# Second passes of the last product: who makes the low parts of the weight sums of steps 1 and 2

## The chip, the cores and the metric

The kernel runs on one core of a Trainium2 chip. The metric is the device time of one launch in microseconds (us). Three timed runs of the kernel before the change took 1035.53, 1036.79 and 1036.57 us, so the median is 1036.57 us. One further execution was profiled; it took 1036.03 us, and its span from first to last instruction is 1034.2 us. All times below that stand in rows of the profile are microseconds from the start of that span.

## The reference

One input `x` (2048 rows of 640) goes through two branches, which are mixed row by row with a gate. Branch A is a Fourier mixing by matrix products, branch B a gated feed-forward layer.

```python
def reference(A_x, A_dft_seq_re, A_dft_seq_im, A_dft_hid_re, A_dft_hid_im, B_x, B_w_gate, B_w_up, B_w_down, gate_w):
    ...
        a = jnp.einsum("bsd,ed->bse", x, dft_hid_re)
        b = jnp.einsum("bsd,ed->bse", x, dft_hid_im)
        y = jnp.einsum("ts,bse->bte", dft_seq_re, a) - jnp.einsum("ts,bse->bte", dft_seq_im, b)
    ...
        return (_gelu(x @ w_gate) * (x @ w_up)) @ w_down
    x = A_x
    g = _sigmoid((x * gate_w).sum(-1, keepdims=True))
    a = _A_ref(x, A_dft_seq_re, A_dft_seq_im, A_dft_hid_re, A_dft_hid_im)
    b = _B_ref(x, B_w_gate, B_w_up, B_w_down)
    return g * a + (1 - g) * b
```

The change touches the last product of branch B, the product of the hidden activations with `w_down` (1728 by 640).

## The kernel before

Nearly every float32 matrix product is made of three matmuls on TensorE. Each operand is split into a high part in the format `fp32r` and a low part, which is what the high part leaves over; `mm3` multiplies high by high (line 99), high weight by low data (line 100) and low weight by high data (line 101). A matmul takes 128 by 128 weights and 128 by 512 data. The products are further arranged in the manner of Strassen: blocks of weights and of data are added and subtracted first, so that fewer products are needed.

The work follows in stages: the gate and up products with the gelu (to about 326 us), the sequence product of branch A (to about 724 us), then the product with `w_down` (724 to 908 us), and last the hidden product of branch A and the mixing. This text is about the third of these.

The product with `w_down` goes over two halves of the output (`tp` 0 and 1), in each over two passes (`b` 0 and 1), and in each pass over steps `k`: six of them (0 to 5) over pairs of blocks of the hidden dimension, and one, `NK` (6), for what is left over. The order in `kseq` is: in pass 0 the steps 0 to 6, in pass 1 the steps 0, 6, 1, 2, 3, 4, 5. Tiles are named by it: `kb0121l` is the low part of the data of half 0, pass 1, step 2, second pair of blocks; `kh` and `kl` are the high and low part of a step's weights, `kw` the weights as loaded, `kr` the data as loaded. Data of step 0 in pass 1 is called `kb0100` and `kb0101`. In the views of the profile numbers at the ends of names are left out.

One iteration of the loop over `kseq` does this: `load_k` of the step three ahead starts the loads (from SyncE's queue: weights `kw` of 128 and 384 KB, then two data tiles `kr` of 512 KB each); `split_k` of the step two ahead makes its high and low parts; `late` carries out what an earlier step left to be gated and stored (line 919 on VectorE, line 920 by a DMA that GpSimd issues); and `step_k` issues the products. In pass 1 the data is not used as loaded: VectorE makes four differences first (lines 826 to 829), 128 by 512 each. Then the high parts of the data are made by ScalarE (line 80) and the low parts by VectorE (line 83).

The weights of pass 1 are loaded as sums made earlier (`wsd`). For these, ScalarE writes the high part (`high`, line 80), then minus the weights into the tile for the low part (`negative`, line 91, which rounds to the same format), and then GpSimd issues a DMA that adds the loaded weights onto it (`left_of`, line 95). In pass 0, `split` does the same with ScalarE for the high part and VectorE for the low one (line 83).

ScalarE and VectorE carry out their work in the order of the program (`in_order`). TensorE, SyncE and GpSimd are set in order by the scheduler of the framework, by its own estimate of when things are ready.

The gate of each half passes through DRAM: sums over rows of `x` on VectorE (line 711), a sigmoid on ScalarE (line 687), a store issued by GpSimd (line 690), and a load of one broadcast row by SyncE (line 695). Loads that stand behind line 695 in SyncE's queue wait with it; those are the loads of steps 1, 2, 3 and on of pass 1.

Of the kernel before, what the change touches and what calls it, by code (L numbers as in the profile page):

```python
# [35 lines left out]
def kernel(  # L36
# [33 lines left out]
    def slot(dt, shape, name):  # L70
        return pool.tile(shape, dt, tag="s4", name=name, bufs=46)
# [7 lines left out]
    def high(hi, raw):  # L79
        nc.scalar.activation(hi, raw, AF.Copy)  # L80

    def low(hi, lo, raw):
        nc.vector.tensor_tensor(lo, raw, hi.bitcast(F32), op=ALU.subtract)  # L83

    def split(hi, lo, raw):
        high(hi, raw)
        low(hi, lo, raw)

    def negative(lo, raw):

        nc.scalar.activation(lo, raw, AF.Copy, scale=-1.0)

    def left_of(lo, raw):

        nc.gpsimd.dma_start(lo, raw, accum_op=ALU.add)
# [41 lines left out]
    def hl(name):  # L137
        return pair(F32R, f"{name}h"), pair(F32R, f"{name}l")

    def at(hilo, i):  # L140
        h, l = hilo
        return h[:, i], l[:, i]
# [676 lines left out]
    def split_k(i):  # L819
        tp, b, k = kseq[i]  # L820
        n = f"{tp}{b}{k}"
        r, raw = kraw.pop(i)
        sums = b and k < NK
        if sums:
            (b11, b12), (b21, b22) = ([v[:, q] for q in range(2)] for v in raw)
            tt(b11, b12, b11, op=ALU.subtract)
            tt(b12, b22, b12, op=ALU.subtract)
            tt(b22, b22, b11, op=ALU.subtract)
            tt(b21, b21, b22, op=ALU.subtract)
        B = []  # L830

        def right():
            B = []
            for q in range(2):
                v = hl(f"kb{n}{q}")
                split(*v, raw[q])
                B += [at(v, 0), at(v, 1)]
            return [B[q] for q in (0, 3, 1, 2)] if sums else B

        if k == NK and b:  # L840
            W = ktile.pop(("left", tp))
        elif k == NK:
            r, m, d = r
            tt(m[:, 5:7], m[:, 0:2], m[:, 2:4], op=ALU.subtract)
            tt(d[:, 0:2], d[:, 0:2], d[:, 2:4], op=ALU.subtract)
            tt(m[:, 5:7], m[:, 5:7], d[:, 0:2], op=ALU.add)
            B = right()
            c, l, a = (slot(F32R, [P, 8, P], f"k{v}{n}") for v in "cla")
            high(c[:, :7], m[:, :7])
            low(c[:, :7], l[:, :7], m[:, :7])  # L850
            high(a[:FR, 2:4], m[:FR, 2:4])
            low(c[FR:, 2:4], a[FR:, 2:4], m[FR:, 2:4])
            x = slot(F32R, [P, 8, P], f"kx{n}")
            split(x[:, 0:2], x[:, 2:4], r[:, 0:2])
            split(x[:, 4], x[:, 5], r[:, 4])
            mx = {"A22": (a[:, 2], a[:, 3])}
            for name, (u, v) in {"A12": (0, 1), "e5": (4, 4), "S4": (5, 6)}.items():
                mx[name] = [[w[q * FR : (q + 1) * FR, k] for w in (c, l)] for q, k in enumerate((u, v))]
            W = {"A11": [(x[:, q], x[:, 2 + q]) for q in range(2)]}, (x[:, 4], x[:, 5]), mx
            kraw["left", tp] = r, m  # L860
            ktile["left", tp] = W
        else:
            h, l = slot(F32R, [P, 8, P], f"kh{n}"), slot(F32R, [P, 8, P], f"kl{n}")
            if b:
                high(h, r)
                negative(l, r)
                left_of(l, r)
            else:
                split(h, l, r)
            names = ("A22", "S1", "S2", "S3") if b else ("A11", "A12", "e5", "S4")  # L870
            W = {name: (at((h, l), 2 * q), at((h, l), 2 * q + 1)) for q, name in enumerate(names)}
        ktile[i] = W, B or right()
# [143 lines left out]
    with in_order(ACT, DVE, PE):  # L1016
# [5 lines left out]
        for d in range(ND):  # L1022
# [3 lines left out]
            if d == 0:  # L1026
                a, b = halves
# [202 lines left out]
    with in_order(PE, ACT, DVE, POOL):  # L1230
        for f in range(1, NF):
# [36 lines left out]
            if f == 2:  # L1268
                k = len(fills) // 2
# [91 lines left out]
    for i, (j, ri, b, sp) in enumerate(cseq):  # L1361
# [70 lines left out]
        else:  # L1432
            if j == 1 and ri == 1 and sp >= 4:
                if sp < 7:
                    load_k(sp - 4)
                if 4 < sp < 7:
                    split_k(sp - 5)
# [55 lines left out]
    for i in range(len(kseq)):  # L1493
# [13 lines left out]
        if i + 2 < len(kseq):  # L1507
            split_k(i + 2)
# [243 lines left out]
```

## Time and profile before

| | |
|---|---|
| median of three timed runs | 1036.57 us |
| profiled execution, time | 1036.03 us |
| profiled execution, span | 1034.2 us |
| mean granted clock of TensorE | 0.993 |
| chain that ended last: TensorE | 90% |
| chain that ended last: DMA `kl<-kw` | 2% |
| HBM read, written | 191.69 MB, 57.69 MB |

The chain that ended last is followed back from the last instruction: at each step to what released it. Its 90% on TensorE says that the time is mostly the sum of the matmuls; its 2% on one DMA, named by output and input, says that somewhere TensorE stood for that transfer. A row of the view by time gives start, duration, engine, line, operation, output and inputs, and in brackets the idle time ahead of it and what ended it. A row of the view by windows gives the stretch, then busy time and number of instructions of PE (TensorE), PEld (its weight loads), DVE (VectorE), ACT (ScalarE) and POOL (GpSimd), then the granted clock, the share in which the DMA engines were busy, and what they moved in GB/s.

### The profile page before, as it was taken

What the parts mean: (1) busy time and instruction counts of PE and PEld (TensorE: products, weight loads), DVE (VectorE), ACT (ScalarE), POOL (GpSimd) and SP (SyncE); (2) the same over time, 40 slices, a digit from 0 to 9 for tenths busy, and PEclk for the clock granted to TensorE, in tenths of its full rate; (3) what the DMA queues carried; (4) which work ended last, traced back from release to release, by engine and by line L of the source; (5) the groups of instructions that cost most, each with busy time, mean ns of one, the idle gap of its engine ahead of it and who ended that gap; (6) DMA issues with size and microseconds to landing.
All of it is one profiled execution on the core that took longest, in us unless ns stands there. A gap on an engine that the chain in (4) does not pass through costs nothing.

```text
span 1034.2 us, 13182 instructions
## 1 busy us (share of the span) xinstructions
PE 1019.9 (99%) x4489; PEld 840.5 (81%) x4489; DVE 813.0 (79%) x1147; ACT 501.6 (48%) x636; POOL 169.3 (16%) x290
## 2 busy tenths in 40 slices
PE   9999999999999999999999999999997999899998
PEld 7888888888888888888888888888886887788887
DVE  8877765564748969978975988777987998797796
ACT  6644535354444744524444444344565637555340
POOL 0221111111110200132023102200211011011112
PEclk9999999999999999999999999999998999899999
DMA  8556364554577976798679768979969999997856
GB/s 310 153 195 219 110 193 132 179 156 153 162 222 251 275 217 211 240 373 299 200 257 397 281 213 285 397 253 312 357 223 330 393 340 347 332 398 220 268 150 99
DMA packets 92164, 261.28 MB, mean 253 GB/s; under 512 B 12160, under 2 KB 22528, under 8 KB 92096
## 3 DMA queue, kind: packets, MB, share of 16 engines
q1 hardware_dynamic: 66624, 180.78, 50.4%
q0 software_dynamic: 25184, 79.46, 26.1%
q8 instruction: 35, 0.57, 0.2%
q14 instruction: 33, 0.27, 0.1%
q10 hardware_dynamic: 288, 0.20, 0.1%
HBM read 191.69 MB, written 57.69 MB: 241 GB/s over the span
## 4 chain that ended last, share of the span: by engine, by line
PE 90%; DMA 3%; issue 3%; DVE 2%; POOL 1%; ACT 0%; SPq 0%; POOLq 0%; DVEq 0%; ACTq 0%
PE pX L101 7%; PE pX L99 7%; PE pX L100 7%; PE pZ L101 5%; PE pZ L100 5%; PE pZ L99 4%; PE pL L99 3%; PE pL L101 3%; PE pL L100 3%; PE pV L99 2%; PE pV L101 2%; PE pV L100 2%; DMA kl<-kw 2%; PE pY L99 1%; PE pR L99 1%
## 5 line engine op out<-in xcount | busy, mean ns | idle before, releaser
L80 ACT ACTIVATE ch<-csa 128x1024 fp32r<-128x1024 f32 x32 | 34.0, 1062 | 79.0 <-DVE csa L767 74.4
L80 ACT ACTIVATE ch<-cra 128x1024 fp32r<-128x1024 f32 x32 | 33.9, 1059 | 46.9 <-DVE cl L83 14.2
L83 DVE TENSOR_TENSOR cl<-cra,ch 128x1024 fp32r<-128x1024 f32 x32 | 39.1, 1222 | 21.0 <-ACT ch L80 18.7
L415 POOL DMA_DIRECT2D hA<-s x48 | 26.2, 546 | 179.3 <-DVE s L582 160.2
L83 DVE TENSOR_TENSOR cl<-crb,ch 128x1024 fp32r<-128x1024 f32 x32 | 39.1, 1221 | 17.2 <-ACT ch L80 15.7
L100 PE MATMUL pL<-cl,xah 128*128 128x512 f32 x128 | 49.8, 389 | 0.0
L101 PE MATMUL pL<-ch,xal 128*128 128x512 f32 x128 | 49.8, 389 | 0.0
L99 PE MATMUL pL<-ch,xah 128*128 128x512 f32 x128 | 49.0, 389 | 0.0
L80 ACT ACTIVATE ch<-crb 128x1024 fp32r<-128x1024 f32 x32 | 33.8, 1057 | 30.6 <-DVE cl L83 8.5
L571 DVE TENSOR_TENSOR s<-s,pX 128x512 f32<-128x512 f32 x24 | 16.4, 684 | 38.5 <-PE pX L101 38.5
L83 DVE TENSOR_TENSOR cl<-csa,ch 128x1024 fp32r<-128x1024 f32 x32 | 39.0, 1220 | 7.2 <-ACT ch L80 5.2
L146 ACT ACTIVATE s<-pX 128x512 f32<-128x512 f32 x41 | 24.2, 596 | 38.2 <-PE pX L101 37.6
L83 DVE TENSOR_TENSOR cl<-csb,ch 128x1024 fp32r<-128x1024 f32 x32 | 39.2, 1224 | 4.2 <-ACT ch L80 3.2
L80 ACT ACTIVATE ch<-csb 128x1024 fp32r<-128x1024 f32 x32 | 34.0, 1063 | 13.5 <-DVE csb L770 5.1
L557 ACT ACTIVATE s<-pZ 128x512 f32<-128x512 f32 x24 | 14.2, 597 | 52.1 <-PE pZ L101 35.3
L576 ACT ACTIVATE s<-s 128x512 f32<-128x512 f32 x24 | 15.1, 634 | 46.6 <-DVE s L575 46.6
L1352 POOL DMA_DIRECT2D uA<-c x8 | 4.3, 540 | 167.1 <-DVE c L1464 166.9
L80 ACT ACTIVATE kh<-kw 128x1024 fp32r<-128x1024 f32 x24 | 25.4, 1058 | 7.6 <-DMA kw<-wsd 7.5
L101 PEld LDWEIGHTS pL<-ch,xal 128*128 128x128 f32 x128 | 24.0, 188 | 5.0
L100 PEld LDWEIGHTS pL<-cl,xah 128*128 128x128 f32 x128 | 24.0, 188 | 5.0
L99 PEld LDWEIGHTS pL<-ch,xah 128*128 128x128 f32 x128 | 24.0, 188 | 5.0
L101 PE MATMUL pX<-ch,xal 128*128 128x512 f32 x64 | 24.9, 389 | 0.0
(3658 smaller groups left out, 3482.3 us busy)
## 6 DMA issues: line engine op xcount, KB each, us to landing
cra<-in_ct SPq DMA_DIRECT2D x64, 512.0 KB, 5.1
crb<-in_ct SPq DMA_DIRECT2D x64, 512.0 KB, 6.0
kr<-hA SPq DMA_DIRECT2D x48, 512.0 KB, 9.2
hA<-s POOLq DMA_DIRECT2D x48, 256.0 KB, 2.9
ux<-uA SPq DMA_DIRECT2D x24, 512.0 KB, 7.3
ux<-uT SPq DMA_DIRECT2D x16, 512.0 KB, 7.0
xq<-xp POOLq DMA_DIRECT2D x12, 512.0 KB, 5.1
xu<-xv POOLq DMA_DIRECT2D x12, 512.0 KB, 4.0
```

The source lines that it names most:

```text
L80: nc.scalar.activation(hi, raw, AF.Copy)
L83: nc.vector.tensor_tensor(lo, raw, hi.bitcast(F32), op=ALU.subtract)
L99: nc.tensor.matmul(ps, lh, rh, start=first, stop=False, skip_group_check=True)
L100: nc.tensor.matmul(ps, lh, rl, start=False, stop=False, skip_group_check=True)
L101: nc.tensor.matmul(ps, ll, rh, start=False, stop=last, skip_group_check=True)
L146: nc.scalar.activation(m, src, AF.Copy)
L415: nc.gpsimd.dma_start(to[:, i], src)
L557: nc.scalar.activation(s5, Z, AF.Copy)
L571: tt(s5, s5, X, op=ALU.add)
L576: nc.scalar.activation(s2, s2, AF.Gelu_apprx_tanh)
L1352: nc.gpsimd.dma_start(to[:, i], src)
```

## The change

In pass 1, steps 1 and 2 of both halves now make the low part of their weights as pass 0 does, with VectorE (`split`). Step 0 and steps 3, 4 and 5 keep ScalarE's negative and the adding DMA.

```diff
@@ -861,7 +861,7 @@
             ktile["left", tp] = W
         else:
             h, l = slot(F32R, [P, 8, P], f"kh{n}"), slot(F32R, [P, 8, P], f"kl{n}")
-            if b:
+            if b and k not in (1, 2):
                 high(h, r)
                 negative(l, r)
                 left_of(l, r)
```

So in all four instructions of line 91 leave ScalarE, four adding DMAs leave GpSimd, and four instructions of line 83 join VectorE.

The order on VectorE, half 0, from the end of the differences of step 1 (`kr0110`, `kr0111`) on. Before:

```order
L829 TENSOR_TENSOR kr0111_6544<-kr0111_6544 128x512
L83 TENSOR_TENSOR kb0110l_6615<-kr0110_6542,kb0110h_6614 128x1024
L83 TENSOR_TENSOR kb0111l_6619<-kr0111_6544,kb0111h_6618 128x1024
L919 TENSOR_TENSOR ks1000_6584<-ks1000_6584,gm5_6507 128x512
L919 TENSOR_TENSOR ks1001_6586<-ks1001_6586,gm5_6507 128x512
L919 TENSOR_TENSOR ksl000_6594<-ksl000_6594,gm5_6507 128x512
L919 TENSOR_TENSOR ksl001_6596<-ksl001_6596,gm5_6507 128x512
L826 TENSOR_TENSOR kr0120_6601<-kr0120_6601 128x512
L827 TENSOR_TENSOR kr0120_6601<-kr0121_6603,kr0120_6601 128x512
L828 TENSOR_TENSOR kr0121_6603<-kr0121_6603,kr0120_6601 128x512
L829 TENSOR_TENSOR kr0121_6603<-kr0121_6603 128x512
L83 TENSOR_TENSOR kb0120l_6677<-kr0120_6601,kb0120h_6676 128x1024
```

And now, from the same place on:

```order
L83 TENSOR_TENSOR kl011_6610<-kw011_6539,kh011_6609 128x1024
L83 TENSOR_TENSOR kb0110l_6614<-kr0110_6542,kb0110h_6613 128x1024
L83 TENSOR_TENSOR kb0111l_6618<-kr0111_6544,kb0111h_6617 128x1024
L919 TENSOR_TENSOR ks1000_6584<-ks1000_6584,gm5_6507 128x512
L919 TENSOR_TENSOR ks1001_6586<-ks1001_6586,gm5_6507 128x512
L919 TENSOR_TENSOR ksl000_6594<-ksl000_6594,gm5_6507 128x512
L919 TENSOR_TENSOR ksl001_6596<-ksl001_6596,gm5_6507 128x512
L826 TENSOR_TENSOR kr0120_6601<-kr0120_6601 128x512
L827 TENSOR_TENSOR kr0120_6601<-kr0121_6603,kr0120_6601 128x512
L828 TENSOR_TENSOR kr0121_6603<-kr0121_6603,kr0120_6601 128x512
L829 TENSOR_TENSOR kr0121_6603<-kr0121_6603 128x512
L83 TENSOR_TENSOR kl012_6671<-kw012_6598,kh012_6670 128x1024
```

The low part of the weights stands ahead of the two low parts of the data, in step 1 (`kl011`) and in step 2 (`kl012`), so all that follows on VectorE stands one and then two instructions further back.

On ScalarE the two rows of line 91 leave, and the next high part moves up. Half 0, steps 1 to 3, before:

```order
L80 ACTIVATE kh011_6609<-kw011_6539 128x1024
L91 ACTIVATE kl011_6610<-kw011_6539 128x1024
L80 ACTIVATE kb0110h_6614<-kr0110_6542 128x1024
L80 ACTIVATE kb0111h_6618<-kr0111_6544 128x1024
L80 ACTIVATE kh012_6671<-kw012_6598 128x1024
L91 ACTIVATE kl012_6672<-kw012_6598 128x1024
L80 ACTIVATE kb0120h_6676<-kr0120_6601 128x1024
L80 ACTIVATE kb0121h_6680<-kr0121_6603 128x1024
L80 ACTIVATE kh013_6717<-kw013_6660 128x1024
L91 ACTIVATE kl013_6718<-kw013_6660 128x1024
```

And now:

```order
L80 ACTIVATE kh011_6609<-kw011_6539 128x1024
L80 ACTIVATE kb0110h_6613<-kr0110_6542 128x1024
L80 ACTIVATE kb0111h_6617<-kr0111_6544 128x1024
L80 ACTIVATE kh012_6670<-kw012_6598 128x1024
L80 ACTIVATE kb0120h_6674<-kr0120_6601 128x1024
L80 ACTIVATE kb0121h_6678<-kr0121_6603 128x1024
L80 ACTIVATE kh013_6715<-kw013_6659 128x1024
L91 ACTIVATE kl013_6716<-kw013_6659 128x1024
```

The negative of step 3 (`kl013`) still stands behind the high parts of step 2's data, which wait for VectorE's differences.

On TensorE the scheduler gives steps 1 and 2 the same order as before, but step 3 another one. The start of step 3, half 0, before:

```order
L99 MATMUL kX000_6201<-kb0131h_6726,kh013_6717 128x512
L100 MATMUL kX000_6201<-kb0131l_6727,kh013_6717 128x512
L101 MATMUL kX000_6201<-kb0131h_6726,kl013_6718 128x512
L99 MATMUL kX001_6202<-kb0131h_6726,kh013_6717 128x512
L100 MATMUL kX001_6202<-kb0131l_6727,kh013_6717 128x512
L101 MATMUL kX001_6202<-kb0131h_6726,kl013_6718 128x512
L99 MATMUL kQ010_6630<-kb0130h_6722,kh013_6717 128x512
```

And now:

```order
L99 MATMUL kX000_6201<-kb0131h_6724,kh013_6715 128x512
L99 MATMUL kX001_6202<-kb0131h_6724,kh013_6715 128x512
L99 MATMUL kQ010_6629<-kb0130h_6720,kh013_6715 128x512
L100 MATMUL kQ010_6629<-kb0130l_6721,kh013_6715 128x512
L99 MATMUL kQ011_6630<-kb0130h_6720,kh013_6715 128x512
L100 MATMUL kX000_6201<-kb0131l_6725,kh013_6715 128x512
L101 MATMUL kX000_6201<-kb0131h_6724,kl013_6716 128x512
```

The first matmul that reads the low part of the weights (`kl013`) stood third in the step and now stands seventh. In step 4 it stood tenth and now stands twelfth; step 5 is as it was, with the low part twelfth. SyncE's loads keep their order. In half 1 all of this is the same.

## The prediction

> **What bounds the kernel now.** First the page's busy times, then the list of TensorE's waits.
>
> ```profile
> PE 1019.9 (99%) x4489; PEld 840.5 (81%) x4489; DVE 813.0 (79%) x1147; ACT 501.6 (48%) x636; POOL 169.3 (16%) x290
> PE kX L101 <- DMA kl<-kw: 10.2, 4, 3.9
> PE idle L1020 <- PEq L1740: 0.8, 1, 0.8
> ```
>
> TensorE is the bound, and but for the start it waits in one place alone: four times, 10.2 us in all, for the adding DMA that makes `kl`. The change acts on that DMA. Its waits in order of time, half 0 and then half 1, each step's first row beside them:
>
> ```profile
> 780.85 0.39 PE L99 MATMUL kX<-kb0111h,kh 128*128 128x512 f32 x1
> 783.10 0.50 PE L101 MATMUL kX<-kb0111h,kl 128*128 128x512 f32 x1 [1.63 <-DMA kl<-kw]
> ...
> 788.23 0.39 PE L99 MATMUL kX<-kb0121h,kh 128*128 128x512 f32 x1
> 792.79 0.79 PE L101 MATMUL kX<-kb0121h,kl 128*128 128x512 f32 x1 [3.94 <-DMA kl<-kw]
> ...
> 800.29 0.39 PE L99 MATMUL kX<-kb0131h,kh 128*128 128x512 f32 x1
> 805.73 0.62 PE L99 MATMUL kQ<-kb0140h,kh 128*128 128x512 f32 x2
> ...
> 873.07 0.39 PE L99 MATMUL kX<-kb1111h,kh 128*128 128x512 f32 x1
> 880.35 0.39 PE L99 MATMUL kX<-kb1121h,kh 128*128 128x512 f32 x1
> 884.00 0.79 PE L101 MATMUL kX<-kb1121h,kl 128*128 128x512 f32 x1 [3.04 <-DMA kl<-kw]
> 891.94 0.39 PE L99 MATMUL kX<-kb1131h,kh 128*128 128x512 f32 x1
> ```
>
> The waits lie in steps 1 and 2, the two that are changed. A step of 24 matmuls without a wait takes 805.73 - 800.29 = 5.44 us, 0.227 a matmul. Step 1 of half 0 takes 788.23 - 780.85 = 7.38, so it loses 1.94; step 2 takes 12.06 and loses 6.62. In half 1 step 1 loses 7.28 - 5.44 = 1.84 and step 2 11.59 - 5.44 = 6.15. That is **16.55 us**, more than the 10.2 of idle time. The rest is in the clock:
>
> ```profile
> 780.78:784.19 3.41, 1.78 (x9) 1.14 (x8) 3.31 (x6) 1.47 (x2) 1.92 (x3) 1.00 1.02 355
> 787.61:791.02 3.41, 1.24 (x6) 0.70 (x4) 3.34 (x4) 2.92 (x3) 0.43 (x1) 1.00 1.06 302
> 791.02:797.85 6.83, 5.06 (x12) 3.99 (x13) 2.49 (x5) 2.00 (x3) 0.86 (x1) 0.50 1.06 289
> 872.94:876.35 3.41, 1.86 (x9) 1.22 (x8) 3.30 (x5) 2.88 (x3) 0.85 (x1) 1.00 1.02 357
> 879.77:883.18 3.41, 1.20 (x6) 0.66 (x4) 3.33 (x4) 2.90 (x3) 0.09 (x1) 1.00 1.03 261
> ```
>
> After each long wait the granted clock is 0.50 for 6.83 us. Of the 3.41 us ahead of that TensorE was busy 1.24 in half 0 and 1.20 in half 1. With 1.78 and 1.86 busy, after the short waits, the clock stayed at 1.00. So a wait of about 1.6 us costs itself alone, one of 3 us costs up to 3.4 us (half of 6.83) on top.
>
> [...]
>
> **The change, part by part.** What it takes from ScalarE and GpSimd is worth nothing by itself, since TensorE never waits for either's busy time. What counts is when VectorE now has `kl`, what it has later for that, and when the next adding DMA, step 3's, lands.
>
> ```profile
> 777.29 1.23 DVE L83 TENSOR_TENSOR kb0111l<-kr,kb0111h 128x1024 fp32r<-128x1024 f32 x1
> ...
> 783.01 0.69 DVE L829 TENSOR_TENSOR kr<-kr 128x512 f32<-128x512 f32 x1
> 784.87 1.22 DVE L83 TENSOR_TENSOR kb0121l<-kr,kb0121h 128x1024 fp32r<-128x1024 f32 x1
> ...
> 807.29 1.22 DVE L83 TENSOR_TENSOR kl<-kw,kh 128x1024 fp32r<-128x1024 f32 x1
> 808.43 1.22 DVE L83 TENSOR_TENSOR kb1000l<-kr,kb1000h 128x1024 fp32r<-128x1024 f32 x1
> 783.78 1.06 ACT L80 ACTIVATE kb0121h<-kr 128x1024 fp32r<-128x1024 f32 x1 [0.44 <-DVE kr L829]
> 785.70 1.04 ACT L91 ACTIVATE kl<-kw 128x1024 fp32r<-128x1024 f32 x1
> 783.36 0.90 POOL L95 DMA_DIRECT2D kl<-kw  x1 [1.41 <-ACT kb0120h L80]
> 787.15 0.89 POOL L95 DMA_DIRECT2D kl<-kw  x1 [2.88 <-PE kR L101]
> 792.54 0.86 POOL L95 DMA_DIRECT2D kl<-kw  x1 [4.50 <-ACT kl L91]
> DMA to landing us min/median/max: 7.7/8.7/9.9
> ```
>
> A low part of a weight tile holds VectorE 808.43 - 807.29 = 1.14 us. *Half 0, step 1:* with `kl` ahead of it, the last data part, begun at 777.29, ends at 777.29 + 1.14 + 1.23 = 779.7, before TensorE asks at 780.85: nothing lost. *Step 2:* its last data part, begun at 784.87 now, comes after two more instructions of 1.14, less the 0.1 it stood for ScalarE: 787.05 to 788.3. TensorE asks for it one matmul into step 2, at 780.85 + 5.44 + 0.23 = 786.5. It waits **1.8 us**, short of the clock's price by the rows above. What VectorE delays behind this (gating, differences) is waited for by step 3 alone.
>
> *Step 3* keeps the adding DMA, and TensorE now comes to it earlier. Its line 91 on ScalarE stands behind `kb0121h`, which waits for VectorE's line 829, now 1.14 later; so 785.70 becomes 786.85. The issue followed line 91's start by 787.15 - 785.70 = 1.45, so it goes out at 788.3. Landings took 7.7 to 9.9 us; I take the median, 8.7: landed at 797.0. TensorE ends step 2 at 788.3 + 23 x 0.227 = 793.5 and by the new order has six matmuls before it reads `kl`, so it asks at 794.9: a wait of **2.1 us** (1.1 to 3.3 over the landings). It leaves TensorE busy for at least 3.4 - 2.1 = 1.3 us of a stretch of 3.4, between the rows with and without the clock's price; I take it without, since a stretch need not begin with the wait. *Step 4:* its issue at 792.54 becomes about 794.5, as VectorE's differences of step 3 are some 2.2 later; landed 803.2, asked for at 797.0 + (18 + 11) x 0.227 = 803.6: hidden, by little. Half 0 gains 8.56 - 1.8 - 2.1 = 4.7.
>
> ```profile
> 866.90 1.23 DVE L83 TENSOR_TENSOR kb1110l<-kr,kb1110h 128x1024 fp32r<-128x1024 f32 x1 [1.32 <-ACT kb1110h L80]
> 875.63 1.23 DVE L83 TENSOR_TENSOR kb1121l<-kr,kb1121h 128x1024 fp32r<-128x1024 f32 x1
> 876.45 1.05 ACT L91 ACTIVATE kl<-kw 128x1024 fp32r<-128x1024 f32 x1
> 877.90 0.89 POOL L95 DMA_DIRECT2D kl<-kw  x1 [1.48 <-ACT kl L91]
> ```
>
> *Half 1* is milder. VectorE stood 1.32 us for `kb1110h`, which was behind line 91 on ScalarE. With that gone, step 1's `kl` fits in the hole and what follows comes 1.32 - 1.14 = 0.2 earlier than before. Step 2 adds 1.14: its last data part ends at 875.63 + 0.94 + 1.23 = 877.8, asked for at 873.07 + 5.44 + 0.23 = 878.7. No wait. Step 3: issue at 877.7, landed 886.4; asked for at 873.07 + 10.88 + 1.36 = 885.3: **1.1 us** (0.1 to 2.3). Steps 4 and 5 follow as in half 0. Half 1 gains 8.0 - 1.1 = 6.9.
>
> *Cover behind.* The time won must not be lost again:
>
> ```profile
> SPq L695 <- DMA gmd<-z: 17.1, 2, 11.5
> 902.36 1.22 DVE L83 TENSOR_TENSOR ub01l<-ux,ub01h 128x1024 fp32r<-128x1024 f32 x1
> 908.26 0.39 PE L99 MATMUL yX<-ub00h,uw00h 128*128 128x512 f32 x1
> 770.00:775.00 5.00, 5.00 (x24) 4.14 (x23) 2.75 (x5) 3.97 (x7) 0.86 (x1) 1.00 1.05 418
> 790.00:795.00 5.00, 2.21 (x5) 1.82 (x6) 1.93 (x3) 2.02 (x3) 0.86 (x1) 0.60 1.05 248
> ```
>
> SyncE stood 17.1 us for the gate's round trip, and the loads of pass 1 stand behind it. In half 1 that round trip hangs on VectorE's row sums; VectorE follows TensorE there through the last sums of half 0, so I shift it with the rest. The next stage has its first data at 903.6, TensorE comes at 908.26: 4.7 us of cover against 6.9 won, but the loads ahead come earlier too. The DMA engines are busy throughout (1.05), at 418 GB/s with little adding under way and 248 with two adding DMAs, so each one taken out brings the queued loads forward. I count neither; the loss is bounded at 6.9 - 4.7 = 2.2 if loads do not move, the gain at the remaining waits, 5.0.
>
> **Sum:** 16.55 - 1.8 - 2.1 - 1.1 = 11.55 us, so 1036.03 - 11.55 = 1024.5 on the profiled execution's own time (1.8 of it lies around the span, which becomes 1022.7). The median of the three runs, 1036.57, is 0.54 above the profiled time; I add half: **1024.7**.
>
> **Rivals.**
> 1. *The clock falls in step 3 too.* Landings of 9.3 us lengthen both waits by 0.6, and half 0's, now 2.7, halves the clock, 3.4 more: 1029.3. With 9.9 and the clock halved in both, 2.4 + 6.8 more: 1033.9. For: the load queue fills the engines. Against: fewer adding DMAs share them.
> 2. *Step 3's DMA lands sooner and nothing is waited for there.* At the best landing, 7.7, half 0 waits 1.1 and half 1 0.1: 1022.7; with no wait in step 3 the sum is 16.55 - 1.8, 1021.5. [...]
> 3. *Slower: step 3's DMA is held back at the issue.* Before, step 2's went out at 783.36, 0.26 after step 1's had landed (TensorE resumed at 783.10), four stores standing between them. If step 3's now waits for those stores, about 791.5, and takes 9.9, it lands at 801.4 and half 0 loses 1.8 + 6.5 + 3.4 = 11.7 against 8.56; half 1, issued as much later (880.9, landed 890.8), loses 5.5 + 3.4 = 8.9 against 8.0: 4.0 us slower, 1040.3. It decides against the change only from where the landings of both halves are together some 4.8 us (11.55 - 6.8) later than forecast, with the clock halved in both. Against: at 787.15 step 3's went out on time behind the same stores and another adding DMA.
> 4. *The wait only moves*, VectorE and the loads setting the pace: both halves keep all but 1 us of the 16.55, 1035.3.
>
> **Chances.** A measurement of this kernel tells some 0.2% (2 us) from no change. Forecast 0.58; rival 1 0.22; rival 2 0.13; rival 3 0.03; rival 4 0.04. So faster 0.93, same 0.04, slower 0.03. Range: from 1020.5 (rival 2 with rounding) to 1031.0, which takes in one halved clock (1029.3) and most of the 2.2 of lost cover with it, and leaves out the clock falling in both halves.
>
> **What would show it.** No wait for `kl` in steps 1 and 2; half 0 a wait of about 1.8 us in step 2 for VectorE's `kb0121l`; waits for the DMA `kl<-kw` in step 3 only, about 2.1 and 1.1 us; no stretch at 0.50 before the end; VectorE's line 83 on `kl` sixteen times instead of twelve, line 95 on `kl` eight. Wrong if the clock drops there, if the stage after 908 or half 1's pass 0 gains a wait, or if step 3's wait is over 3 us.

## The result, and the profile after

The changed kernel takes **1026.07 us** (median of 4 runs, 1025.56 to 1026.69), against 1036.05 us for the kernel before in the same session (1034.91 to 1036.79, 4 runs). The ratio is **0.9905, 95% interval 0.9888 to 0.9922**. The prediction was 1024.7 us, in a range of 1020.5 to 1031.0: the direction is as forecast, and the time lies 1.4 us above it (11.9 us were to be won, 10.0 were). The profiled execution took 1026.28 us, its span is 1024.5 us: 9.7 us less than the 1034.2 of before.

The page's busy times of the changed kernel:

```profile
PE 1015.3 (99%) x4489; PEld 836.8 (82%) x4489; DVE 816.3 (80%) x1151; ACT 497.2 (49%) x632; POOL 165.4 (16%) x286
```

And its list of TensorE's waits (engine, output, line, what was waited for; us in total, times, the longest):

```profile
PE kX L101 <- DMA kl<-kw: 2.2, 2, 1.6
PE kX L100 <- DVE kb0121l L83: 1.5, 1, 1.5
PE yZ L99 <- DVE ksa L978: 1.0, 1, 1.0
PE idle L1020 <- PEq L1740: 0.8, 1, 0.8
```

The 10.2 us of waits for the adding DMA have become 2.2 for the DMA, 1.5 for VectorE and, new, 1.0 at the start of the next stage. Where they lie, in order of time (start, duration, engine, line, operation; in brackets the idle time and what ended it):

```profile
786.60 0.39 PE L99 MATMUL kX<-kb0121h,kh 128*128 128x512 f32 x1
...
788.53 0.50 PE L100 MATMUL kX<-kb0121l,kh 128*128 128x512 f32 x1 [1.54 <-DVE kb0121l L83]
...
793.90 0.61 PE L99 MATMUL kX<-kb0131h,kh 128*128 128x512 f32 x2
...
797.04 0.50 PE L101 MATMUL kX<-kb0131h,kl 128*128 128x512 f32 x1 [1.62 <-DMA kl<-kw]
...
801.26 0.62 PE L99 MATMUL kQ<-kb0140h,kh 128*128 128x512 f32 x2
...
868.71 0.39 PE L99 MATMUL kX<-kb1111h,kh 128*128 128x512 f32 x1
...
881.68 0.50 PE L101 MATMUL kX<-kb1131h,kl 128*128 128x512 f32 x1 [0.57 <-DMA kl<-kw]
...
896.81 0.39 PE L99 MATMUL yX<-ub00h,uw00h 128*128 128x512 f32 x1
...
899.35 0.50 PE L99 MATMUL yZ<-ub01h,uw00h 128*128 128x512 f32 x1 [1.01 <-DVE ksa L978]
```

Half 1's step 1 starts at 868.71 instead of 873.07 (4.36 us won in half 0), and the next stage at 896.81 instead of 908.26: **11.45 us won** by then. The span is only 9.7 shorter, so about 1.75 us are given back behind 896.81. Most of that goes at once: the first 60 matmuls of the next stage take 13.60 us in the kernel before (908.26 to 921.86) and 15.06 in the changed one (896.81 to 911.87), 1.46 us more. The adding DMAs of step 3, half 0 and half 1:

```profile
788.54 0.91 POOL L95 DMA_DIRECT2D kl<-kw  x1 [5.26 <-ACT kl L91]
...
873.28 0.92 POOL L95 DMA_DIRECT2D kl<-kw  x1 [5.28 <-PE kR L101]
```

The first landed at 796.99 by the trace, 8.46 us after its issue, just ahead of the matmul at 797.04. What is waited for at 899.35 is on VectorE:

```profile
893.99 1.22 DVE L83 TENSOR_TENSOR uw02l<-uw02r,uw02h 128x1024 fp32r<-128x1024 f32 x1 [0.62 <-ACT uw02h L80]
895.14 1.22 DVE L83 TENSOR_TENSOR ub10l<-ux,ub10h 128x1024 fp32r<-128x1024 f32 x1
896.27 1.22 DVE L83 TENSOR_TENSOR ub11l<-ux,ub11h 128x1024 fp32r<-128x1024 f32 x1
897.41 1.29 DVE L978 TENSOR_TENSOR ks<-ks,ks 128x512 f32<-128x512 f32 x2
898.61 1.28 DVE L978 TENSOR_TENSOR ksa<-ks,kQ 128x512 f32<-128x512 f32 x2
```

Line 978 adds up the last pass of the `w_down` product and so empties the PSUM banks (`kQ`) that the next stage's `yZ` takes. In VectorE's order it stands behind the low parts of data that is needed later (`uw02`, `ub10`, `ub11`). TensorE, earlier than it used to be, now comes before the banks are empty.

### The profile page after: what moved, and what is told of

The parts are those of the page before. It is cut to its first block, busy times and chain, and to the rows that moved or that the text cites. A ratio compares the mean times of both kernels' runs of the same rounds, so it can differ in the third digit from the quotient of the medians.

```text
span 1024.5 us, 13176 instructions
## 1 busy us (share of the span) xinstructions
PE 1015.3 (99%) x4489; PEld 836.8 (82%) x4489; DVE 816.3 (80%) x1151; ACT 497.2 (49%) x632; POOL 165.4 (16%) x286
## 4 chain that ended last, share of the span: by engine, by line
PE 82%; DMA 8%; DVE 6%; issue 2%; ACT 1%; SPq 0%; DVEq 0%; ACTq 0%
PE pX L99 7%; PE pX L101 7%; PE pX L100 7%; PE pZ L101 5%; PE pZ L100 5%; PE pZ L99 5%; DMA kw<-wsd 4%; PE pL L100 3%; PE pL L99 3%; PE pL L101 3%; PE pV L100 2%; PE pV L99 2%; PE pV L101 2%; PE pY L100 1%; PE pR L100 1%
```

## The experiments

All times are medians; the kernel before took 1035.66 us beside the first four runs, 1035.67 beside the next four and 1035.97 beside the last three.

| run | time, us | ratio, 95% interval |
|---|---|---|
| e1_step1_alone | 1035.09 | 0.9993 (0.9984 to 1.0003) |
| e2_step2_alone | 1031.12 | 0.9956 (0.994 to 0.9971) |
| e3_dma_traffic_back | 1036.37 | 1.0006 (0.9996 to 1.0015) |
| e4_evict_first | 1024.32 | 0.9886 (0.9869 to 0.9903) |
| e5_spare_negative | 1026.25 | 0.9909 (0.9894 to 0.9924) |
| e6_spare_plain_dma | 1031.67 | 0.9964 (0.9951 to 0.9977) |
| e7_hoist_step3 | 1024.85 | 0.9898 (0.9883 to 0.9913) |
| e8_hoist_and_defer | 1023.53 | 0.9884 (0.9867 to 0.99) |
| e9_step3_too | 1027.06 | 0.9913 (0.9898 to 0.9928) |
| e10_step3_too_ordered | 1025.68 | 0.9897 (0.9882 to 0.9912) |
| e11_empty_first_both | 1023.60 | 0.9881 (0.9864 to 0.9897) |

### One step of the two (e1, e2)

```diff
-            if b and k not in (1, 2):
+            if b and k != 1:
```

> Only step 1 of pass 1 makes its low part of the weights by VectorE; step 2 keeps ScalarE's negative and the adding DMA. Theory (what counts is when the low part of step 2 is there, since its wait cost 6.62 and 6.15 us of the 16.55): TensorE no longer waits in step 1 and so comes to step 2 some 1.9 us earlier, where the adding DMA, now issued right behind the four stores at about 783.6, lands at about 792.3. Half 0 loses 5.2 us there and 2.4 to 3.4 more by the halved clock, half 1 2.3 to 5.7. Time about 1032 us (1030 to 1034). Rival 1 (the gain comes from taking adding DMAs off the DMA engines, each worth the same): half of the gain, 1031. Rival 2 (step 1's wait is the cause of step 2's): nearly the whole gain, 1027.

```diff
-            if b and k not in (1, 2):
+            if b and k != 2:
```

> Only step 2 makes its low part of the weights by VectorE; step 1 keeps the adding DMA. Theory: step 1 waits as before the change (1.9 and 1.8 us), which gives VectorE time, so that step 2 waits for nothing, and step 3's adding DMA is asked for later and is waited for by 1 us in half 0 and not in half 1. Losses 2.9 and 1.8 against 3.9 and 0.9 with the whole change: the same time, 1026 us (1025 to 1027.5). Rival 1 (DMA engines): half of the gain, 1031. Rival 2 (step 1's wait is the cause): close to before, 1034 or more.

Step 1 alone is worth nothing that can be told from no change. Its waits are gone, but step 2 waits longer. Its waits for the DMA:

```profile
PE kX L101 <- DMA kl<-kw: 10.5, 2, 6.1
```

And the windows ahead of the long wait's end in half 0 and behind it:

```profile
787.49:790.90 3.41, 0.49 (x1) 0.17 (x1) 3.31 (x5) 2.23 (x3) 0.88 (x1) 0.99 1.05 352
790.90:797.73 6.83, 3.60 (x9) 2.84 (x10) 6.58 (x8) 5.60 (x7) 0.87 (x1) 0.50 1.05 287
```

Two waits instead of four, but 10.5 us of them instead of 10.2, and the clock still halved for 6.83 us after each. Step 2's adding DMA goes out at 783.51, as the expectation had it (783.6), but lands 10.6 us later, at 794.08 instead of 792.3; in half 1 it took 10.9. That is why the 1032 us expected did not come. Rival 4 of the prediction ("the wait only moves") is right for this half of the change.

Step 2 alone is worth 4.5 us; 1026 was expected, and 1031 by the rival that set the DMA engines first. Its waits:

```profile
PE kX L101 <- DMA kl<-kw: 3.4, 2, 1.9
PE yX L99 <- ACT ks L146: 2.1, 1, 2.1
PE yZ L99 <- DVE ksa L978: 1.3, 1, 1.3
PE kZ L99 <- DVE ksa L978: 0.9, 1, 0.9
```

Step 1's adding DMA (3.4 us, and the clock halved once, for 3.41 us) explains one part. The other stands at the two hand-overs, from half 0 to half 1 (`kZ`) and from half 1 to the next stage (`yX`, `yZ`): 4.3 us, where the kernel before had no wait and the changed kernel 1.0. `ks` of line 146 is ScalarE's copy that empties the first banks. This speaks for the DMA engines, and the next three runs test that.

### What the two adding DMAs cost (e3, e5, e6)

The whole change, with the removed work put back into a tile that nothing reads:

```diff
             else:
                 split(h, l, r)
+                if b:
+                    spare = slot(F32R, [P, 8, P], f"ky{n}")
+                    negative(spare, r)
+                    left_of(spare, r)
```

> As the whole change, but steps 1 and 2 also write the negative on ScalarE and issue the adding DMA, into a tile that nobody reads: the work on ScalarE, GpSimd and the DMA engines is that of before, only that TensorE takes the low part from VectorE. Theory: no wait in step 1, about 1.9 us in step 2 as with the change; step 3's adding DMA, with another one under way, lands 0.8 us later in half 0 and up to 1.5 later in half 1: 1028.5 us, up to 1032 if the clock is halved there. Rival 1 (the gain comes from less on the DMA engines): the gain is gone, 1035 to 1036. A third, that ScalarE's four instructions are what counts: also 1035 to 1036.

It took 1036.37 us, the time of its rival 1 and not the theory's 1028.5: **the whole gain is gone**, though VectorE makes the low parts as in the changed kernel, and no engine reads the spare tile. TensorE's longest waits in e3 (the clock is also halved twice, for 3.41 us from 888.73 and from 905.80):

```profile
PE kX L101 <- DMA kl<-kw: 4.9, 3, 2.0
PE yX L99 <- ACT ks L146: 1.8, 1, 1.8
PE kX L99 <- ACT ks L146: 1.3, 1, 1.3
PE kZ L99 <- DVE ksa L982: 0.9, 1, 0.9
```

ScalarE's work ahead of the next stage in e3, in order of time:

```profile
896.55 1.06 ACT L80 ACTIVATE uw00h<-uw00r 128x1024 fp32r<-128x1024 f32 x1 [5.18 <-DMA uw00r<-wsu]
...
901.77 1.06 ACT L80 ACTIVATE uw02h<-uw02r 128x1024 fp32r<-128x1024 f32 x1 [0.89 <-DMA uw02r<-wsu]
902.74 1.04 ACT L80 ACTIVATE ub10h<-ux 128x1024 fp32r<-128x1024 f32 x1
903.68 1.04 ACT L80 ACTIVATE ub11h<-ux 128x1024 fp32r<-128x1024 f32 x1
904.63 1.06 ACT L146 ACTIVATE ks<-kX 128x512 f32<-128x512 f32 x2
```

The same two of these in the changed kernel:

```profile
887.48 1.05 ACT L80 ACTIVATE uw00h<-uw00r 128x1024 fp32r<-128x1024 f32 x1
...
895.76 1.06 ACT L146 ACTIVATE ks<-kX 128x512 f32<-128x512 f32 x2
```

This is the chain: the loads land later (ScalarE stands 5.18 us for `uw00r`), ScalarE works in order, its copy that empties the banks stands behind those splits, 8.9 us later, and TensorE stands at the hand-over. Half 0 to half 1 goes the same way.

One load does wait for a spare DMA itself. In half 1 SyncE stands at the load of `ux`, with that of `uw00r` next behind it, until the DMA issued at 865.47 has landed at 874.32:

```profile
SPq L1336 <- DMA ky<-kw: 3.9, 1, 3.9
```

All these tiles share one pool of 46 buffers (`slot`), and by this wait a buffer that the spare DMA read or wrote was not free before it had landed. So a part of e3's loss may be this hold and not the traffic; the kernel before had such a wait too, of 1.3 us, for `kl<-kw`.

The run put back three things: ScalarE's negative, the DMA, and the tile's space. Two more take these apart: the tile with `negative(spare, r)` alone, and the tile with a plain `nc.gpsimd.dma_start(spare, r)` alone.

> The whole change, plus ScalarE's negative copy of steps 1 and 2 into a tile that nothing reads; no adding DMA is put back. Theory (what took the gain away in the run with both put back is the two adding DMAs' share of the DMA engines, which delays the queued loads): 1026, within 1 us of the changed kernel, and 374 GB/s in 770:810 and 860:900. Rival (ScalarE's 1.04 us a copy, or the tile's slot in SBUF, delays ScalarE's emptying of the PSUM banks and so the hand-over): 1031 to 1036.

> The whole change, plus in steps 1 and 2 a plain DMA of the same 512 KB into the unread tile, from the same GpSimd queue, without adding, and without ScalarE's negative. If an adding DMA costs the engines its bytes alone, this costs what the adding one did: 1036. If adding makes it dearer than its bytes (the windows' 347 GB/s with and 374 without two of them say some 3 us of all engines each, where 512 KB at 374 GB/s is 1.4 us), about half of the loss comes back: 1030 to 1032. If the traffic was not the cause at all: 1026.

With the negative and the tile the time is 1026.25, as without them, and the rate below is 374 GB/s as well; TensorE's waits lie elsewhere (3.4 us for the adding DMA in five places, none at the last hand-over). With a plain DMA it is 1031.67, and there no load waits for a spare DMA, by the trace; TensorE stands at the last hand-over all the same:

```profile
PE yX L99 <- ACT ks L146: 2.9, 1, 2.9
```

So the traffic alone cost time here, 5.42 us (1031.67 against 1026.25); what the hold adds to it in e3 was not separated. Each run has four such DMAs of 512 KB: the plain one cost (1031.67 - 1026.25) / 4 = 1.36 us of the kernel's time, the adding one (1036.37 - 1026.25) / 4 = 2.53, both against e5 (the kernel before, beside e3 and beside e5, differed by 0.01). The second includes e3's hold and its two halved stretches. What the DMA engines move shows the traffic by itself. From 770 to 810 us, in the kernel before, the changed kernel, e3 and e6:

```profile
770.00:810.00 40.00, 34.42 (x140) 27.62 (x139) 31.60 (x39) 24.85 (x27) 6.64 (x9) 0.91 1.04 347
```

```profile
770.00:810.00 40.00, 36.84 (x161) 29.64 (x161) 37.11 (x45) 26.41 (x30) 4.83 (x7) 1.00 1.04 374
```

```profile
770.00:810.00 40.00, 36.42 (x158) 29.00 (x157) 33.30 (x41) 25.05 (x27) 6.63 (x9) 1.00 1.05 347
```

```profile
770.00:810.00 40.00, 36.39 (x159) 29.16 (x157) 34.84 (x42) 24.48 (x27) 6.00 (x9) 1.00 1.04 366
```

The engines are busy throughout in all four (the last but one figure, 1.04 to 1.05); the rate (the last) is 347 GB/s in the two kernels in which all adding DMAs run, and 374 in the one without two of them; e6's 366 counts the plain DMAs' own bytes. The 1.36 us of the plain DMA are, as nearly as these times tell, its 512 KB at 374 GB/s (524288 / 374000 = 1.40). The packets say what the adding one cost on the engines. GpSimd's queue from 770 to 900 us in e5, e3 and e6 (packets, MB, the time that its packets took as a share of the 16 engines' time):

```profile
q0 software_dynamic: 2192, 7.35, 21.2%
```

```profile
q0 software_dynamic: 2768, 9.45, 29.3%
```

```profile
q0 software_dynamic: 2770, 9.45, 25.4%
```

Beyond e5, four adding DMAs took 8.1% of the 130 us, 2.63 us of all engines each, and four plain ones 4.2%, 1.37 each: the adding one cost **1.9 times** the plain one. That the kernel's time gives nearly the same two prices is in part chance, as e3's holds more than the traffic. What the engines do in the additional time no run here shows.

### The time given back at the next stage (e4)

```diff
-        if m > 0:
+        def split_more():
             for p in ((0, 1), (2,))[m - 1]:
                 split_uw(0, p)
             split_u(m - 1)
+        if m == 1:
+            split_more()
...
         step_k(i)
+        if m == 2:
+            split_more()
```

In the last step of the `w_down` product this places line 978 ahead of the splits of `uw02`, `ub10` and `ub11`.

> As the whole change, but in the last step of the product with w_down the splits for the next stage (line 83 on uw02, ub10, ub11) stand behind the sums that empty the PSUM banks (line 978), not ahead of them. Theory: TensorE's wait of 1.0 us at the start of the next stage (yZ, for VectorE's ksa, line 978), with 0.2 to 0.4 behind it, is the gain that came back as a new wait; it goes, and the time is about 1.2 us shorter than with the change, 1024.9. Rival: the wait only moves to the data ub10 that is now made later, and the time is the same, 1026.

1024.32 us; the wait for `ksa` is gone from the list. In this run line 978 with `kQ` starts at 895.65 instead of 898.61:

```profile
895.65 1.28 DVE L978 TENSOR_TENSOR ksa<-ks,kQ 128x512 f32<-128x512 f32 x2
```

So most of what was given back went to VectorE's order at the hand-over. The first 60 matmuls of the next stage take 13.60 us in e4 (896.33 to 909.93), as before the change, so it is worth 1.46 us. The medians differ by 1.75 (1026.07 - 1024.32) and the spans by 1.9 (1024.5 - 1022.6); most of the rest lies ahead of this edit, as e4 also comes to step 1 of half 0 0.37 us earlier (780.79 instead of 781.16).

### The waits that are left (e7, e8)

ScalarE stands idle for 5.13 us ahead of step 2's data parts in half 0. `by_dma` holds the high copy, the negative and the adding DMA, and is called for the next step there; e7 does so for step 3, on top of e4:

```diff
+            if b and k in (2,):
+                early[i + 1] = hl3 = tuple(slot(F32R, [P, 8, P], f"k{c}{tp}{b}{k + 1}") for c in "hl")
+                by_dma(*hl3, kraw[i + 1][0])
```

> The change with the banks emptied first at the last hand-over, and ScalarE's two copies and the adding DMA of step 3 moved ahead of step 2's data parts (ScalarE stands idle for 5.1 us there). Theory (the wait left in step 3 is the adding DMA's issue, 788.54, plus its 8.5 us, and the time before the next stage has cover again): both waits of step 3 go, 1.6 and 0.6 us or so: 1022.1 (1021.5 to 1023). Rival (step 3 then waits for VectorE's data parts instead, or the hand-over takes it): 1024.3. Second rival (two adding DMAs closer together slow the loads): 1026.

1024.85 us, no better than e4. The rival's time is near (1024.3), but its places are not: the gain is not lost at VectorE's data parts or at the hand-over. The adding DMA goes out 5 us earlier, at 783.52, and step 3 waits for nothing, but step 4 does:

```profile
803.25 0.50 PE L101 MATMUL kX<-kb0141h,kl 128*128 128x512 f32 x1 [1.94 <-DMA kl<-kw]
```

Step 4's adding DMA went out at 794.73, as in the changed kernel (794.71), while TensorE came to step 4 2.6 us earlier (798.65 instead of 801.26). The traced execution, 1024.35 us, kept the clock; two others, at a mean clock of 0.998, took 1025.14 and 1025.84. In the prediction step 4 was "hidden, by little", and so it was.

e8 does it for steps 3, 4 and 5 (`k in (2, 3, 4)`), and puts VectorE's gating (line 919) behind step 2's low parts:

```diff
-        late()
+        if i not in (7, 21):
+            late()
```

> As the run before, with the copies and adding DMAs of steps 3, 4 and 5 each moved a step ahead, and VectorE's gating (line 919, 2.4 us) put behind step 2's low parts. Theory: the wait for VectorE's kb0121l, 1.6 us, goes too: 1020.5 (1019.5 to 1022). Rival 1 (the next wait is for loads or for VectorE's data parts a step later, which the 2.4 us now delay): 1022 to 1024. Rival 2 (three adding DMAs go out closer together, land later, up to 10.9 us, and are waited for in steps 4 and 5): 1026 or more.

**1023.53 us**, with e11 the best of all runs. The steps have almost no waits left; the longest is at the hand-over to half 1:

```profile
PE kZ L99 <- DVE ksa L988: 1.7, 1, 1.7
...
PE kX L99 <- ACT kb0131h L80: 0.3, 1, 0.3
```

Of its expectations rival 1 comes nearest: the wait for VectorE goes, and the next one is on VectorE, though at the hand-over and not for data parts. Against e4 it wins 0.8 us, and the two intervals overlap, so its lead over e4 is not certain.

### Further in the same direction (e9, e10, e11)

```diff
-            if b and k not in (1, 2):
+            if b and k not in (1, 2, 3):
```

> The change carried one step further and nothing else: steps 1, 2 and 3 by VectorE, steps 4 and 5 by the adding DMA. Theory (DMA engines relieved bring the loads forward, and VectorE's later low parts cost what TensorE then waits for them): the waits of step 3 go, 1.6 and 0.9; VectorE's last data part of step 3 ends 1.14 later, at 794.8, asked for at 794.1, so 0.7 back; one more adding DMA fewer in each half brings the loads of the hand-overs forward, where 1.4 were lost: 1024.5 (1023 to 1026). Rival (VectorE, busy 37 of 40 us there, becomes the bound, and its emptying of the banks at the hand-overs is late): 1027 to 1030.

1027.06 us, the rival's lower end, but for another reason than VectorE alone. Step 3 still waits 0.45 us for VectorE, and the adding DMAs of steps 4 and 5 are now the late ones:

```profile
PE kX L101 <- DMA kl<-kw: 3.4, 3, 1.7
```

e10 is e8 with step 3 on VectorE as well, and steps 4 and 5 hoisted:

> Steps 1, 2 and 3 by VectorE; the banks emptied first at the last hand-over; line 919 behind step 2's low parts; the copies and adding DMAs of steps 4 and 5 a step ahead. Against the best so far, 1023.53, it has one adding DMA fewer in each half and 1.14 us more on VectorE. Theory: the 1.7 us that are left at the first hand-over stand on VectorE's splits, and these now come 1.14 later: 1024 to 1025. Rival (the loads are what the hand-over waits for): 1022.5 or less.

1025.68 us, somewhat worse than the theory's 1024 to 1025. The steps are nearly free of waits, and `kZ` at the hand-over waits 2.06 us for line 988, which here halved the clock for 3.41 us: 0.4 us more than e8's wait there and 1.7 for the clock (half of 3.41) are nearly all of the 2.15 us by which it is behind e8. The one execution that kept the clock took 1024.28. One adding DMA fewer in each half no longer pays: VectorE, in order, is what the hand-over waits for.

e11 is e8 with the banks emptied first at the hand-over to half 1 too:

```diff
-        if i + 2 < len(kseq):
+        if i + 2 < len(kseq) and i != 13:
             split_k(i + 2)
...
         step_k(i)
+        if i == 13:
+            split_k(i + 2)
```

> As the run of 1023.53, and at the hand-over from half 0 to half 1 too the banks are emptied before the next step's splits. Theory: the 1.7 us for kZ and 0.7 for kV shrink to about 1.5 together, but the next step's low parts on VectorE, 3.4 us, come 6 us later, at 818, and its matmuls ask at 815: it loses 2 to 3 us there: 1024.5 to 1026. Rival (the next step has cover enough): 1022.5.

1023.60 us, the same as e8. Neither time is right: the next step did have cover, as the rival says, and the next stage starts 1.5 us earlier (893.94 instead of 895.41 by the traces), but the span is 1021.8 in both. What it won is lost at once at the last hand-over: the stage's first 60 matmuls take 15.16 us (to 909.10) instead of 13.64, with 0.9 us of waits for line 988 (`yV` 0.7, `yZ` 0.2) among them.

## Why the prediction was right, and where it was short

**The loss before, 16.55 us in steps 1 and 2.** Right: those waits and both stretches of halved clock are gone.

**Step 1, both halves; step 2, half 1: no wait.** Right.

**Step 2, half 0: a wait of 1.8 us for VectorE.** It was 1.54, and the step took 7.30 us (786.60 to 793.90), 1.86 above 5.44. The wait cost some 0.3 more than its idle time, as in step 1 before the change (1.63 of wait, 1.94 lost).

**Step 3: waits of 2.1 and 1.1 us.** 1.62 and 0.57; the steps took 7.36 and 6.34 us, 1.92 and 0.90 above 5.44. The issue in half 0 (forecast 788.3) was at 788.54 and the landing (797.0) at 796.99; TensorE came at 795.4 rather than 794.9. **Step 4 hidden:** right, and e7 shows how little there was to spare.

**The clock stays up.** Right: no stretch at 0.50 before the end. Here luck had a part. In the 3.41 us from 794.92, which hold the wait of 1.62, TensorE was busy for 1.79, and the last section shows a halved clock behind 1.63; the 2.1 us of the forecast would have left it open.

**Won by the next stage's start:** 11.55 forecast, 11.45 measured. Half 0 gave 4.36 (forecast 4.7; 4.67 from the start of its step 1, which came 0.31 later, at 781.16), half 1 7.09 (6.9).

**Cover behind** is the term that was mis-sized. The prediction bounded the loss there at 2.2 us, set it against the loads coming earlier, and counted neither; 1.75 was lost, 1.46 of it at the hand-over, and the next stage gained a wait, which the prediction itself had named as a sign of being wrong. It also looked at the wrong thing: it measured the cover by when the stage's first data is ready (`ub01l`), which was in time. What was late is the emptying of the banks, which TensorE needs just as much; e4 shows it.

**"What it takes from ScalarE and GpSimd is worth nothing by itself"** is the sentence that falls. For ScalarE it holds, by the time of e5. For the adding DMAs it does not: the sum was built on when VectorE has `kl`, and e3 has VectorE on time and gains nothing. Taking the adding DMAs off the busy DMA engines is needed for the gain; what that would be worth without the earlier low parts no run shows. The prediction had it among the remarks ("each one taken out brings the queued loads forward"), and the sum came out nearly right, by luck in this point, because the relief and the earlier need for the loads went together. With the relief taken back, the hand-overs, which had cover in the kernel before, and the later adding DMAs are what TensorE waits for.

**Rivals.** 1 did not happen (step 3's waits were shorter than forecast). 2 lies near by its number alone: both waits were shorter by 0.5 (what they cost, by 0.2), though the DMA landed on time and TensorE was later. 3 and 4 did not happen to the whole change; 4 is what step 1 alone does.

## What to carry to other kernels

A transfer that nothing waits for can still cost its time. Here, with the DMA engines busy throughout (1.04 to 1.05 from 770 to 810 us), 512 KB took 1.37 us of all engines by a plain DMA (e6) and 2.63 by an adding one (e3), and the kernel was 1.36 and 2.53 us longer for each, paid at the loads behind them (in e3 ScalarE stood 5.18 us for `uw00r`). In e3 a buffer also stayed taken until the spare DMA had landed, and a load stood 3.9 us for that. So price a removed transfer by what it holds up, not by its own wait. When TensorE is to come earlier to a stage, list everything it needs there, the emptied PSUM banks as well as the data, and look in the order of each engine at what stands ahead of them. An edit that frees one step of a chain of like steps should be tried on its neighbours together: alone, step 1 gave nothing and step 3's hoist moved the wait to step 4.

## What the runs showed of the hardware that was not expected

In these runs the clock did not go by the length of a wait alone. e3 halved it after a wait of 1.79 us and e2 after one of 1.9, while e7 (1.94 us) and e6 (2.9 us at `yX`) kept it. The halved stretches ahead of the kernel's end are 3.41 us long (e2, e3) or 6.83 (the kernel before, e1), and in two runs their starts lie on a grid: in the kernel before 791.02 and 883.18 are 92.16 apart, 27 times 3.413, and in e3 888.73 and 905.80 are 17.07 apart, 5 times 3.414. Read by that grid, drawn back for each run from a start of a halved stretch, the busy time of TensorE in a window went with the clock of the next. The window ahead and the next one, in e2 and in e3:

```profile
782.43:785.85 3.42, 1.52 (x8) 1.25 (x8) 3.32 (x5) 2.22 (x3) 0.43 (x1) 1.00 1.02 385
785.85:789.26 3.41, 3.41 (x10) 2.65 (x9) 3.38 (x4) 1.79 (x2) 0.90 (x1) 0.50 1.03 418
```

```profile
902.38:905.80 3.42, 1.63 (x7) 1.05 (x6) 3.07 (x4) 3.42 (x6) 0.00 (x0) 1.00 1.04 417
905.80:909.21 3.41, 2.94 (x7) 1.82 (x6) 3.41 (x6) 2.73 (x3) 0.00 (x0) 0.50 1.03 420
```

And in e6, where the 2.9 us fall into two windows; this is the second, with part of a wait of 1.3 for `yZ` in it as well:

```profile
901.08:904.49 3.41, 1.66 (x6) 1.05 (x6) 3.41 (x5) 3.41 (x5) 0.00 (x0) 1.00 1.04 417
904.49:907.91 3.42, 2.47 (x11) 1.88 (x11) 3.42 (x7) 1.27 (x2) 0.00 (x0) 1.00 1.02 417
```

In the windows read in this way, those at full clock with 0.49 to 1.63 us busy were followed by 0.50 (e1 0.49, the kernel before 1.20 and 1.24, e3 1.42 and 1.63, e2 1.52), and those with 1.66 or more by 1.00 (e6 1.66, the kernel before 1.78 and 1.86, the changed kernel 1.79). One with 1.63 (e7, 801.46 to 804.88) kept the clock as well, so the profile's busy time alone does not separate the two. The author's estimate from these few rows is that where the waits of 1.8 to 2.9 us fell in the grid decided whether they cost clock. At half clock 1.64 and 2.58 us busy (the kernel before, from 791.02 and from 883.18) were followed by 0.50 again, 2.94 (e3, above) by 1.00. Why the clock goes this way no run shows.

The second thing is the price of an adding DMA on the engines, 1.9 times that of a plain one (2.63 us of all engines for 512 KB in e3 against 1.37 in e6), told above. Its time to landing for the same 512 KB was 7.8 to 9.2 us in the changed kernel, but up to 10.9 in e1; what makes these longer was not tried.
